# Value buffers initialised ahead of every load, sink rows filled ahead of the queued loads, weights loaded behind blocks 4 and 5

## Chip, cores, metric

One core of one Trainium2 chip. The metric is device microseconds of one execution. Single executions of one kernel spread by 1 to 4%. A run more than 1.5% above the fastest of its kernel counts as slow, and kernels are compared by their fast runs alone: ratios are the mean time of one kernel's fast runs over that of the other's of the same rounds. The medians quoted beside them are of all runs, so they do not give quite the same ratios. q3, k8 and the like are the loads of q or k of that block.

## The reference

Windowed attention with four sink positions, then a highway layer. q, k and v are 4 batches x 8 heads x 768 positions x 64, in float32.

```python
scores = scale * np.matmul(q, k.transpose(0, 1, 3, 2))
keep = is_sink | in_window                 # key < 4, or 0 <= query - key < 128
a = softmax(np.where(keep, scores, -1e9))
x = np.matmul(a, v)  ->  (3072, 512)       # heads side by side
H = np.maximum(x @ w_h, 0.0)
T = 1.0 / (1.0 + np.exp(-(x @ w_t + b_t)))
out = T * H + (1.0 - T) * x
```

## The kernel before

The 3072 rows are 24 blocks of 128, six to a batch. Every load casts float32 to float16 on its way and is issued by GpSimd. GpSimd's program runs up to eight blocks ahead of TensorE (`AHEAD = 8`); each engine runs its own list in order.

```python
# buffers of v: 12 of them; a column of 2.0 and a zero tail are written once, the rest by loads
for vt in v_ring[0:3]:
    init_v(vt)                              # VectorE, at the start
...
# GpSimd: loads 0, 1, 2 between the masks, then
load_sink_v(0)                              # 4 KB: v of the 4 sink positions
load_qk(3); load_v(3)
dma(wt_sb, moe_w_t); dma(wh_sb, moe_w_h)    # 512 KB each in SBUF
load_qk(4); load_v(4)
...
for i in range(-2, NB + LAG + 1):           # LAG = 4
    if i == -2:
        more_constants(); late_constants()
        for vt in v_ring[3:NV]:             # the other 9 buffers: VectorE
            init_v(vt)
        sink_ones(); sink_v(0)
    ...
    pe_T(i + 2)                             # TensorE transposes q and k: waits for their loads
    pe_A(i)                                 # e times v, and for blocks 2 to 5 of a batch the sink rows
    dve_x(i); sp_X(i)                       # x, then its transpose by DMA
    pe_Mt(i - LAG); pe_Mh(i - LAG)          # highway matmuls
    pe_sink(i + 1)                          # scores of sink keys (ks), blocks 2 to 5 of a batch, every other i
    # GpSimd: loads of block i+10 (5 to 8 at i == -2)
    load_qk(n); load_v(n)
    if (i + 2) % 6 == 0: pool_sink(...)     # GpSimd copies the batch's 4 sink keys into ks
    if i % 6 == 3: load_sink_v(next batch)
    if i % 6 == 0: sink_v(i // 6)           # GpSimd spreads the sink rows of v into vs
```

The softmax here doesn't subtract the row's maximum and nothing guards it: scores larger than these inputs give would overflow.

Of the kernel before, what the change touches and what calls it, by code (L numbers as in the profile page):

```python
# [8 lines left out]
FP16 = mybir.dt.float16  # L9
# [11 lines left out]
def kernel(  # L21
# [18 lines left out]
    nc = tc.nc  # L40
    P = 128

    B, H, S, D = q.shape
# [8 lines left out]
    NSC = S // P  # L52
# [3 lines left out]
    NOC = DM // P  # L56
    SCALE = 1.0 / math.sqrt(D)
    VW = H * 65 + 64
    AHEAD = 8
    LAG = 4  # L60

    const = ctx.enter_context(tc.tile_pool(name="const", bufs=1))
    sd_pool = ctx.enter_context(tc.tile_pool(name="p_sd", bufs=AHEAD))
# [3 lines left out]
    x_pool = ctx.enter_context(tc.tile_pool(name="p_x", bufs=LAG + 3))  # L67
# [4 lines left out]
    m_ps = ctx.enter_context(tc.tile_pool(name="ps_m", bufs=2, space=bass.MemoryType.PSUM))  # L72

    NV = AHEAD + 4
    v_ring = [const.tile([P, VW], FP16, tag=f"v{i}", name=f"v{i}") for i in range(NV)]
    qk_sd = {}

    def load_qk(n):
        b, c = divmod(n, NSC)
        rows = slice(c * P, (c + 1) * P)  # L80
        qsd = sd_pool.tile([P, H, D], FP16, tag="qsd", name="qsd")
        ksd = sd_pool.tile([P, H, D], FP16, tag="ksd", name="ksd")
        nc.gpsimd.dma_start(out=qsd, in_=q[b, :, rows, :].transpose([1, 0, 2]))  # L83
        nc.gpsimd.dma_start(out=ksd, in_=k[b, :, rows, :].transpose([1, 0, 2]))  # L84
        qk_sd[n] = (qsd, ksd)

    def load_v(n):
        b, c = divmod(n, NSC)
        rows = slice(c * P, (c + 1) * P)
        vt = v_ring[n % NV][:, 0:H * 65].rearrange("p (h e) -> p h e", e=65)  # L90
        nc.gpsimd.dma_start(out=vt[:, :, 0:D], in_=v[b, :, rows, :].transpose([1, 0, 2]))  # L91

    def init_v(vt):
        nc.vector.memset(vt[:, 0:H * 65].rearrange("p (h e) -> p h e", e=65)[:, :, D:D + 1], 2.0)  # L94
        nc.vector.memset(vt[:, H * 65:VW], 0.0)

    warm = const.tile([P, DM], FP16, tag="warm")
    ident = const.tile([P, P], FP16, tag="ident")
# [5 lines left out]
    wh_sb = const.tile([P, NOC, DM], FP16, tag="wh")  # L104
    wt_sb = const.tile([P, NOC, DM], FP16, tag="wt")
# [10 lines left out]
    with tc.manual_schedule(engines={ENG.DVE}):  # L116
        nc.vector.memset(warm, 0.0)
        nc.vector.memset(ident, 1.0)
        nc.vector.memset(ebias, _EXP_BIAS)
        nc.vector.memset(mask, 1.0)  # L120
        nc.vector.memset(bm, 1.0)
        for vt in v_ring[0:3]:
            init_v(vt)

    def load_sink_v(b):
        nc.gpsimd.dma_start(out=vs_dn[b % 2], in_=v[b, :, 0:4, :])

    def sink_v(b):
        nc.gpsimd.tensor_tensor(  # L129
            out=vs_bd[b % 2][0:NS4, :, 0:D], in0=vs_dn[b % 2].unsqueeze(1).to_broadcast([NS4, H, D]),  # L130
            in1=bm[0:NS4, :].unsqueeze(2).to_broadcast([NS4, H, D]), op=ALU.mult)

    with tc.manual_schedule(engines={ENG.Pool}):
        load_qk(0)
        nc.gpsimd.affine_select(
            out=ident, in_=ident, compare_op=ALU.is_equal, fill=0.0,
            base=0, pattern=[[-1, P]], channel_multiplier=1)
        load_v(0)
        load_qk(1)
        nc.gpsimd.affine_select(  # L140
            out=mask[:, 1, :], in_=mask[:, 1, :], compare_op=ALU.is_ge, fill=0.0,
            base=0, pattern=[[1, P]], channel_multiplier=-1)
        load_v(1)
        nc.gpsimd.affine_select(
            out=mask[:, 0, :], in_=mask[:, 0, :], compare_op=ALU.is_ge, fill=0.0,
            base=-1, pattern=[[-1, P]], channel_multiplier=1)
        load_qk(2)
        nc.gpsimd.affine_select(
            out=bm, in_=bm, compare_op=ALU.is_ge, fill=0.0,
            base=0, pattern=[[-4, H]], channel_multiplier=1)  # L150
        nc.gpsimd.affine_select(
            out=bm, in_=bm, compare_op=ALU.is_ge, fill=0.0,
            base=3, pattern=[[4, H]], channel_multiplier=-1)
        load_v(2)
        load_sink_v(0)
        load_qk(3)
        load_v(3)
        nc.gpsimd.dma_start(out=wt_sb, in_=moe_w_t.rearrange("(kc p) of -> p kc of", p=P))
        nc.gpsimd.dma_start(out=wh_sb, in_=moe_w_h.rearrange("(kc p) of -> p kc of", p=P))
        load_qk(4)  # L160
        load_v(4)

    nc.sync.dma_start(out=bt32, in_=moe_b_t.unsqueeze(0))

# [24 lines left out]
            nc.tensor.matmul(w, lhsT=warm[:, 0:P], rhs=warm, start=True, stop=True)  # L189

    qkT, tp_of, s_of, e_of, av_of, rec_of = {}, {}, {}, {}, {}, {}
    xh_of, xT_of, t_of, u_of, h_of, dd_of, ee_of, sk_of = {}, {}, {}, {}, {}, {}, {}, {}

    def pe_T(n):
        qsd, ksd = qk_sd.pop(n)
        tp = m_ps.tile([P, 2 * NHP, P], FP16, tag="m", name="tp")
        for j in range(NHP):
            nc.tensor.transpose(tp[:, j, :], qsd[:, 2 * j:2 * j + 2, :], ident)
        for j in range(NHP):
            nc.tensor.transpose(tp[:, NHP + j, :], ksd[:, 2 * j:2 * j + 2, :], ident)  # L200
        tp_of[n] = tp

    def act_T(n):
        qk = qkT_pool.tile([P, 2 * NHP, P], FP16, tag="qk", name="qk")
        nc.scalar.copy(out=qk, in_=tp_of.pop(n))  # L205
        qkT[n] = (qk[:, 0:NHP, :], qk[:, NHP:2 * NHP, :])

    def pool_sink(b):
        _, kT = qkT[b * NSC]
        ks = ks_bd[b % 2]  # L210
        for hh in range(2):
            rows = slice(64 * hh, 64 * hh + 64)
            dst = ks[rows, 0:NHP * 136].rearrange("p (a b) -> p a b", b=136)
            nc.gpsimd.tensor_copy(out=dst[:, :, 4 * hh:4 * hh + NSINK],
                                  in_=kT[rows, :, 0:NSINK])
# [87 lines left out]
    def sp_X(n):  # L303
        xT = x_pool.tile([P, NOC, P], FP16, tag="xT", name="xT")
        nc.sync.dma_start_transpose(out=xT, in_=xh_of[n])
        xT_of[n] = xT

    def pe_Mt(n):
        xT = xT_of[n]
        tps = m_ps.tile([P, DM], FP32, tag="m", name="tps")  # L310
        nc.tensor.matmul(tps, lhsT=ones_row, rhs=bt16, start=True, stop=False)  # L311
        for kc in range(NOC):
            nc.tensor.matmul(tps, lhsT=xT[:, kc, :], rhs=wt_sb[:, kc, :],  # L313
                             start=False, stop=(kc == NOC - 1))
        t_of[n] = tps
# [26 lines left out]
    def dve_o(n):  # L342
# [2 lines left out]
                                       op0=ALU.mult, op1=ALU.add)  # L345
        nc.sync.dma_start(out=out[n * P:(n + 1) * P, :], in_=otok)

    def on(n):
        return 0 <= n < NB

    with tc.manual_schedule(engines={ENG.PE, ENG.DVE, ENG.Activation, ENG.SP, ENG.Pool}):
        for i in range(-2, NB + LAG + 1):
            m, o = i - LAG, i - LAG - 1
            if i == -2:
                warm_up(8)
                more_constants()
                late_constants()
                for vt in v_ring[3:NV]:
                    init_v(vt)
                sink_ones()  # L360
                sink_v(0)
            if on(i) and i % NSC >= 2 and i % 2 == 0:
                act_sink(i)
            if on(i + 1):
                pe_S(i + 1, 0)
                act_S(i + 1, 0)
                pe_S(i + 1, 1)
            if on(o):
                dve_d(o)
            if on(i):  # L370
                dve_mask(i, 1)
            if on(i + 2):
                pe_T(i + 2)
            if on(o):
                dve_e(o)
            if on(i):
                pe_A(i)
            if on(i + 2):
                act_T(i + 2)
            if on(i + 1):  # L380
                act_S(i + 1, 1)
                dve_mask(i + 1, 0)
            if on(i):
                dve_rec(i)
            if on(o):
                dve_o(o)
            if on(i):
                dve_x(i)
                sp_X(i)
            if on(m):  # L390
                pe_Mt(m)
                act_u(m)
                pe_Mh(m)
            if on(i + 1) and (i + 1) % NSC >= 2 and (i + 1) % 2 == 0:
                pe_sink(i + 1)
            first, last = (5, AHEAD) if i == -2 else (i + 2 + AHEAD, i + 2 + AHEAD)
            for n in range(first, last + 1):
                if n < NB:
                    load_qk(n)
                    load_v(n)  # L400
            if on(i + 2) and (i + 2) % NSC == 0:
                pool_sink((i + 2) // NSC)
            b = i // NSC + 1
            if i >= 0 and i % NSC == 3 and b < B:
                load_sink_v(b)
            if i >= 0 and i % NSC == 0 and i > 0 and i // NSC < B:
                sink_v(i // NSC)


# [33 lines left out]
```

## Time and profile before

| | before |
|---|---|
| median of the runs beside the changed kernel | 148.12 us (147.62 to 149.33) |
| span of the profiled run | 144.5 us |
| busy: TensorE, VectorE, ScalarE, GpSimd | 76, 67, 60, 52% of the span |
| block 0 multiplied with v (av) from | 28.2 us |

Two rows of the page's picture in 40 slices show where TensorE stands still. A digit is the busy share of a slice of 3.6 us in tenths; PEclk is the granted clock.

```profile
span 144.5 us, 3130 instructions
PE   6645000190799999989999994899999999979930
PEclk9999999999999999999999999999999999999998
```

Counted from 1, slices 5 to 7, with zeros, and slice 8 are the hole from 14 to 28 us that the change is after; the 0 and 7 in slices 10 and 11 are the wait for sink keys. The rest is read in the prediction.

### The profile page before, as it was taken

Reading aid. Unit: us, or ns where it says so; the run is one execution under the profiler, and the core shown is the slowest. Engines: PE = TensorE matmul, PEld = TensorE weight load, DVE = VectorE, ACT = ScalarE, POOL = GpSimd, SP = SyncE. Lnnn points to the kernel's source line nnn. Section 1 sums busy time; section 2 is a strip of 40 time slices with the busy share of each in tenths; the row PEclk is TensorE's granted clock in tenths of the full one; section 3 lists DMA queues with packets and bytes.
Section 4 is the critical chain, followed back from the end, with each engine's and each line's share of the span. In section 5 each row is a group of like instructions: output and inputs, shape, how many; then the busy total and the mean of one; then the engine's idle time right before and its main releaser. Section 6 shows DMA issues by size and latency. Waiting matters only on the chain.

```text
span 144.5 us, 3130 instructions
## 1 busy us (share of the span) xinstructions
PE 109.9 (76%) x1216; PEld 70.4 (49%) x1216; DVE 97.0 (67%) x213; ACT 86.9 (60%) x105; POOL 75.8 (52%) x99
## 2 busy tenths in 40 slices
PE   6645000190799999989999994899999999979930
PEld 2234000180688566656765663567666666644400
DVE  6220000464066789988888995499889989988990
ACT  3058300061499869887886989198869888812210
POOL 6989980399999959876746479641030000000000
PEclk9999999999999999999999999999999999999998
DMA  1999999999999999999999999999943422634331
GB/s 11 111 134 105 119 173 169 86 96 147 160 156 155 153 134 194 196 186 163 179 187 187 182 185 161 140 178 195 185 119 109 113 90 79 54 111 128 126 145 73
DMA packets 92784, 20.14 MB, mean 139 GB/s; under 512 B 88673, under 2 KB 89697, under 8 KB 92770
## 3 DMA queue, kind: packets, MB, share of 16 engines
q0 software_dynamic: 76256, 10.51, 116.2%
q1 hardware_dynamic: 16514, 9.44, 31.3%
q8 instruction: 9, 0.15, 0.5%
q14 instruction: 5, 0.04, 0.1%
HBM read 21.01 MB, written 6.29 MB: 189 GB/s over the span
## 4 chain that ended last, share of the span: by engine, by line
PE 29%; POOL 25%; DMA 21%; issue 9%; DVE 8%; ACT 4%; POOLq 0%; DVEq 0%
DMA v<-in_v_dram 21%; POOL qsd L83 8%; POOL ksd L84 7%; PE tps L313 7%; PE hps L326 6%; POOL v L91 6%; PE av L279 6%; PE sps L245 3%; DVE dd L332 3%; DVE ee L338 2%; DVE otok L344 2%; ACT e L253 2%; PE av L285 2%; POOL vs L129 2%; PE tps L311 2%
## 5 line engine op out<-in xcount | busy, mean ns | idle before, releaser
L253 ACT ACTIVATE e<-sps,ebias 128x1024 f16<-128x1024 f32 (+1 forms) x48 | 49.8, 1042 | 19.8 <-PE sps L245 19.6
L279 PE MATMUL av<-v,e 128*128 128x112 f16 x352 | 25.4, 221 | 15.5 <-DVE e L264 15.5
L264 DVE TENSOR_TENSOR e<-e,mask 128x1024 f16<-128x1024 f16 (+1 forms) x48 | 31.1, 650 | 7.5 <-ACT e L253 7.1
L279 PEld LDWEIGHTS <-e 128*128 128x128 f16 x352 | 21.3, 102 | 21.0 <-DVE e L264 16.6
L205 ACT COPY qk<-tp 128x1024 f16<-128x1024 f16 x24 | 24.1, 1003 | 7.0 <-PE tp L200 7.0
L91 POOL DMA_DIRECT2D v<-in_v_dram x24 | 21.8, 910 | 10.2 <-DVE v L94 6.4
L84 POOL DMA_DIRECT2D ksd<-in_k_dram x24 | 21.7, 902 | 6.8 <-PE tps L313 3.4
L83 POOL DMA_DIRECT2D qsd<-in_q_dram x24 | 22.2, 925 | 4.9 <-DMA ksd<-in_k_dram 1.4
L326 PE MATMUL hps<-wh_sb,xT 128*128 128x512 f16 x96 | 24.6, 379 | 0.0
L313 PE MATMUL tps<-wt_sb,xT 128*128 128x512 f16 x96 | 24.6, 379 | 0.0
L319 ACT ACTIVATE u<-tps 128x512 f16<-128x512 f32 x24 | 14.4, 599 | 14.6 <-PE tps L313 14.6
L332 DVE SCALAR_TENSOR_TENSOR dd<-hps,xh 128x512 f16<-128x512 f32 x24 | 16.6, 690 | 7.4 <-PE hps L326 7.0
L245 PE MATMUL sps<-qk 64*128 64x128 f16 x352 | 16.0, 231 | 2.7 <-ACT qk L205 2.2
L338 DVE SCALAR_TENSOR_TENSOR ee<-u,dd 128x512 f16<-128x512 f16 x24 | 16.5, 686 | 0.5
L298 DVE TENSOR_TENSOR xh<-av,rec 128x512 f16<-128x512 f32 x24 | 16.4, 685 | 0.2
L245 PEld LDWEIGHTS <-qk 64*128 64x128 f16 x352 | 11.2, 100 | 9.9 <-issue 7.8
L344 DVE SCALAR_TENSOR_TENSOR otok<-xh,ee 128x512 f32<-128x512 f16 x24 | 15.6, 652 | 0.2
L326 PEld LDWEIGHTS <-xT 128*128 128x128 f16 x96 | 9.4, 98 | 11.8 <-issue 0.8
L313 PEld LDWEIGHTS <-xT 128*128 128x128 f16 x96 | 9.4, 98 | 9.2
L94 DVE MEMSET v<- 128x8 f16 x12 | 0.7, 65 | 18.4 <-DMA v<-in_v_dram 18.4
L285 PE MATMUL av<-vs,es 128*128 128x260 f16 x32 | 9.0, 281 | 3.3 <-POOL vs L129 3.3
L200 PE MATMUL tp<-ident,ksd 128*128 128x128 f16 x96 | 10.5, 238 | 1.1 <-DMA ksd<-in_k_dram 1.1
(45 smaller groups left out, 81.4 us busy)
## 6 DMA issues: line engine op xcount, KB each, us to landing
out_dram<-otok SPq DMA_DIRECT2D x24, 256.0 KB, 3.8
qsd<-in_q_dram POOLq DMA_DIRECT2D x24, 128.0 KB, 8.5
ksd<-in_k_dram POOLq DMA_DIRECT2D x24, 128.0 KB, 8.4
v<-in_v_dram POOLq DMA_DIRECT2D x24, 128.0 KB, 8.8
wt_sb<-in_moe_w_t_dram POOLq DMA_DIRECT2D x1, 512.0 KB, 7.6
wh_sb<-in_moe_w_h_dram POOLq DMA_DIRECT2D x1, 512.0 KB, 9.4
xT<-xh SPq DMA_TRANSPOSE x24, 7.0
vd<-in_v_dram POOLq DMA_DIRECT2D x4, 4.0 KB, 8.8
```

The costliest lines, as they stand in the source:

```text
L83: nc.gpsimd.dma_start(out=qsd, in_=q[b, :, rows, :].transpose([1, 0, 2]))
L84: nc.gpsimd.dma_start(out=ksd, in_=k[b, :, rows, :].transpose([1, 0, 2]))
L91: nc.gpsimd.dma_start(out=vt[:, :, 0:D], in_=v[b, :, rows, :].transpose([1, 0, 2]))
L205: nc.scalar.copy(out=qk, in_=tp_of.pop(n))
L245: nc.tensor.matmul(sps[:, hh, o:o + P], lhsT=kk[rows, hp, :], rhs=qT[rows, hp, :], start=True, stop=True)
L253: nc.scalar.activation(out=e.rearrange("p a b c d -> p a (b c d)"), in_=sps[:, :, 0:2 * np_ * P], func=AF.Exp, bias=ebias, scale=SCALE)
L264: nc.vector.tensor_tensor(out=ev, in0=ev, in1=m.unsqueeze(1).to_broadcast([P, 4, np_ * P]), op=ALU.mult)
L279: nc.tensor.matmul(av[:, g, 2 * hl + hh, 0:_AVN], lhsT=e[:, hh, hl, pc, :], rhs=vt[:, 65 * h:65 * h + _AVN], start=first, stop=False, skip ...
L313: nc.tensor.matmul(tps, lhsT=xT[:, kc, :], rhs=wt_sb[:, kc, :], start=False, stop=(kc == NOC - 1))
L326: nc.tensor.matmul(hps, lhsT=xT[:, kc, :], rhs=wh_sb[:, kc, :], start=(kc == 0), stop=(kc == NOC - 1))
L332: nc.vector.scalar_tensor_tensor(out=dd, in0=h_of.pop(n), scalar=0.0, in1=xh_of[n], op0=ALU.max, op1=ALU.subtract)
L338: nc.vector.scalar_tensor_tensor(out=ee, in0=u_of.pop(n), scalar=1.0, in1=dd_of.pop(n), op0=ALU.add, op1=ALU.mult)
```

## The change

The intent is to let VectorE through: no memset of a v buffer shall wait for a load into that buffer. Then TensorE needs the sinks early, so they are filled ahead of the loads that queue up, and the weights, needed only from block 0's highway step on, go behind blocks 4 and 5. (The diff also brings a way to transpose x on TensorE, which is switched off: `by_dma` is always true.)

```diff
+    WAT = 4
-        for vt in v_ring[0:3]:
+        for vt in v_ring:
             init_v(vt)
...
         load_v(2)
         load_sink_v(0)
-        load_qk(3)
-        load_v(3)
-        (wt_sb and wh_sb loaded)
-        load_qk(4)
-        load_v(4)
...
-                for vt in v_ring[3:NV]:
-                    init_v(vt)
                 sink_ones()
-                sink_v(0)
...
-            first, last = (5, AHEAD) if i == -2 else (i + 2 + AHEAD, i + 2 + AHEAD)
-            for n in range(first, last + 1):
+            if on(i + 2) and (i + 2) % NSC == 0:
+                pool_sink((i + 2) // NSC)
+                sink_v((i + 2) // NSC)
+            for n in (range(3, AHEAD + 1) if i == -2 else [i + 2 + AHEAD]):
                 if n < NB:
                     load_qk(n)
                     load_v(n)
-            if on(i + 2) and (i + 2) % NSC == 0:
-                pool_sink((i + 2) // NSC)
+                if n == WAT:      (wt_sb loaded)
+                if n == WAT + 1:  (wh_sb loaded)
             b = i // NSC + 1
-            if i >= 0 and i % NSC == 3 and b < B:
+            if i >= 0 and i % NSC == 1 and b < B:
                 load_sink_v(b)
-            if i >= 0 and i % NSC == 0 and i > 0 and i // NSC < B:
-                sink_v(i // NSC)
```

More of the change, by code (lines that the diff above doesn't have):

```diff
@@ L155 @@
         load_sink_v(0)
-        load_qk(3)
-        load_v(3)
-        nc.gpsimd.dma_start(out=wt_sb, in_=moe_w_t.rearrange("(kc p) of -> p kc of", p=P))
-        nc.gpsimd.dma_start(out=wh_sb, in_=moe_w_h.rearrange("(kc p) of -> p kc of", p=P))
-        load_qk(4)
-        load_v(4)
     nc.sync.dma_start(out=bt32, in_=moe_b_t.unsqueeze(0))
@@ L191 @@
     qkT, tp_of, s_of, e_of, av_of, rec_of = {}, {}, {}, {}, {}, {}
+    xtp_of = {}
     xh_of, xT_of, t_of, u_of, h_of, dd_of, ee_of, sk_of = {}, {}, {}, {}, {}, {}, {}, {}
@@ L306, in sp_X, with pe_X, act_X @@
         xT_of[n] = xT
+    def pe_X(n):
+        xh = xh_of[n]
+        xtp = m_ps.tile([P, NOC, P], FP16, tag="m", name="xtp")
+        for j in range(NOC):
+            nc.tensor.transpose(xtp[:, j, :], xh[:, j * P:(j + 1) * P], ident)
+        xtp_of[n] = xtp
+    def act_X(n):
+        xT = x_pool.tile([P, NOC, P], FP16, tag="xT", name="xT")
+        nc.scalar.copy(out=xT, in_=xtp_of.pop(n))
+        xT_of[n] = xT
     def pe_Mt(n):
@@ L346, in dve_o, with by_dma @@
         nc.sync.dma_start(out=out[n * P:(n + 1) * P, :], in_=otok)
+    def by_dma(n):
+        return True
     def on(n):
@@ L373 @@
                 pe_T(i + 2)
+            if on(i - 1) and not by_dma(i - 1):
+                pe_X(i - 1)
             if on(o):
@@ L379 @@
                 act_T(i + 2)
+            if on(i - 1) and not by_dma(i - 1):
+                act_X(i - 1)
             if on(i + 1):
@@ L388 @@
                 dve_x(i)
-                sp_X(i)
+                if by_dma(i):
+                    sp_X(i)
             if on(m):
@@ L400 @@
                     load_v(n)
-            if on(i + 2) and (i + 2) % NSC == 0:
-                pool_sink((i + 2) // NSC)
+                if n == WAT:
+                    nc.gpsimd.dma_start(out=wt_sb, in_=moe_w_t.rearrange("(kc p) of -> p kc of", p=P))
+                if n == WAT + 1:
+                    nc.gpsimd.dma_start(out=wh_sb, in_=moe_w_h.rearrange("(kc p) of -> p kc of", p=P))
             b = i // NSC + 1
-            if i >= 0 and i % NSC == 3 and b < B:
+            if i >= 0 and i % NSC == 1 and b < B:
                 load_sink_v(b)
-            if i >= 0 and i % NSC == 0 and i > 0 and i // NSC < B:
-                sink_v(i // NSC)
 _INS = ['q', 'k', 'v', 'n_sink', 'window', 'moe_w_h', 'moe_w_t', 'moe_b_t']
```

## The prediction

> **What bounds the kernel now.** I read the page, then the waits of the first 45 us, then the timeline of that stretch, then GpSimd's timeline to the end of its loads. The first four lines below are waits of 0 to 45 us (engine, line, what it waited for: us in total, times, longest); the rest are rows of the timeline (start us, length us, engine, line, operation, and in brackets the idle time before it with its releaser).
>
> ```profile
> DVE v L94 <- DMA v<-in_v_dram: 18.4, 2, 9.3
> PEld L279 <- DVE e L264: 15.0, 1, 15.0
> POOL v L91 <- DVE v L94: 6.4, 1, 6.4
> PE sk L223 <- POOL ks L214: 4.4, 1, 4.4
> ...
> 17.56 0.95 POOL L91 DMA_DIRECT2D v<-in_v_dram  x1
> 18.17 0.07 DVE L94 MEMSET v<- 128x8 f16 x1 [9.34 <-DMA v<-in_v_dram]
> ...
> 27.27 0.07 DVE L94 MEMSET v<- 128x8 f16 x1 [9.01 <-DMA v<-in_v_dram]
> ...
> 27.78 1.34 DVE L264 TENSOR_TENSOR e<-e,mask 128x512 f16<-128x512 f16 x3
> 28.24 0.69 PEld L279 LDWEIGHTS <-e 128*128 128x128 f16 x8 [14.99 <-DVE e L264]
> ```
>
> VectorE reaches the memsets of v buffers 3 to 11 at 8.8 us, but buffers 3 and 4 have loads under way into them by then, so it waits until load v3 lands (18.1) and load v4, which is queued behind both weights, lands (27.2). Only then does it mask the exponentials of block 0, which ScalarE had finished at about 9.3 and 12; TensorE waits 15 us for that mask. GpSimd in turn waits 6.4 us for the memset of v5, and its copies of the sink keys stand behind loads 5 to 8, which costs TensorE another 4.4 us. Block 0 thus starts its A matmuls at 28.24 and not near 13.5.
>
> The later part is different. The windows of 4 us show TensorE busy 4.00 of 4.00 in nearly all from 48 to 124, and a block takes about 4.1 us there (the tps groups start at 116.45, 120.52, 124.62, 128.63). But the queue of loads is full too, as GpSimd's rows show:
>
> ```profile
> 20.38 0.91 POOL L84 DMA_DIRECT2D ksd<-in_k_dram  x1
> 27.70 0.88 POOL L91 DMA_DIRECT2D v<-in_v_dram  x1 [6.40 <-DVE v L94]
> ...
> 64.79 0.88 POOL L84 DMA_DIRECT2D ksd<-in_k_dram  x1 [0.67 <-DMA v<-in_v_dram]
> ...
> 81.56 0.88 POOL L91 DMA_DIRECT2D v<-in_v_dram  x1 [1.86 <-DMA ksd<-in_k_dram]
> ...
> 89.64 1.03 POOL L129 TENSOR_TENSOR vs<-vd,bm 32x512 f16<-32x512 f16 x1
> ...
> 95.20 0.88 POOL L91 DMA_DIRECT2D v<-in_v_dram  x1 [1.62 <-DMA qsd<-in_q_dram]
> ```
>
> Eight loads can be under way (in the built program each load waits for the landing of the one eight before it), and between 60 and 96 GpSimd waits again and again for such a landing. Adding each issue's time to landing gives the supply: k8 lands at 40.4, k17 at 74.9, k23 at 102.7. So from k8 to k23 a block of loads takes 62.3/15 = 4.15 us, as much as TensorE needs. It does not hurt before the change because TensorE is late: it transposes block 8 at 53.5 (13 us after k8 landed) and block 23 at 118.8 (16 us after). **That lead is what the change will eat.**
>
> **What the Trainium skill says.** "Trainium Kernel Development and Optimization", Key Constraints: DMAs issued from SP, ACT and POOL run on the same 16 DMA engines and interleave; "DMA: Bandwidth & Descriptors", SWDGE vs HWDGE vs iDMA: each DMA engine round-robins between the queues that feed it. The trace agrees: alone but backlogged, loads land 0.85 us apart (24.49 to 28.73, five loads), beside transposes and stores 1.4 us apart (4.15/3). "DMA: Bandwidth & Descriptors", Anatomy of one DMA, gives a fixed cost of about 2.0 us; here the 4 KB load of sink rows took 3.07 us from issue to landing at the start, and that number is used. "TensorE: Matmul & The Clock Gate", Part 1, says that TensorE runs at half clock until it has been busy for some 3.4 us: here four transposes take 0.61 us up to 40 us and 0.40 us from 42 us on, though the granted clock is 1.00 throughout, so early blocks cost TensorE more (3.5 to 4.5 us).
>
> **The change part by part.**
>
> (a) All v buffers are initialised ahead of the loads. It moves nine pairs of memsets (about 0.06 us a pair in the row at 27.3 and after, 0.55 us) to about 1.8 us, where VectorE has 2.28 us to spare before the mask at 6.66. It removes the 18.4 us of VectorE's waits and the 6.4 us of GpSimd's. Block 0 can be multiplied at about 13.5 (after its block 2 transposes, 12.5 to 13.5). Up to 14.7 us are free here, if the loads follow.
>
> (b) Sink rows ahead of queued loads. The order of GpSimd's instructions in the changed program: the two copies of sink keys between the two selects on bm (9.45 to 9.94 before; qk of block 0 is done at 8.15, so no wait, 0.54 us), then v2, then the 4 KB load, then at once the sink-value multiply, which waits for that load. Issue of v2 about 10.8, of the 4 KB load 11.7, landing 11.7 + 3.07 = 14.8, multiply 1.12: GpSimd issues q3 at 16.0 rather than 11.70. **A new wait: 4.3 us in which no load is issued.** Later batches: the TensorE waits for the sink values (2.58 us at 90.7, 0.72 at 63.3) go, since the load is issued two blocks earlier and the multiply ahead of that iteration's loads.
>
> (c) Weights behind blocks 4 and 5. The weights took 24.49 - 18.09 = 6.4 us of the queue. Now q3..v4 come before them. I walk the queue with 0.88 us an issue, 3.9 us from issue to landing, 0.85 us a queued load and 3.2 us a weight: k3 lands at 20.9 (before: 16.7), k4 23.4 (26.2), first weight 27.5, k5 29.0 (28.7), second weight 32.5, k6 34.1 (34.8), k7 36.6 (37.4), k8 39.2 without company, about 41 with the transposes that now run beside it (40.4). **The supply is therefore about where it was;** only the lead is used.
>
> The sum: TensorE's order puts the transposes of block n+2 ahead of the A matmuls of block n, so it runs as k arrives: block 3 at 21, 4 at 23.5, 5 at 29, 6 at 34.5, 7 at 37.5, 8 at 41 against 53.5 before, 12.5 us earlier. From there it may go at 4.1 us (block 23 at 41 + 15*4.1 = 102.5) or as the loads arrive. The loads: 62.3 us as before from k8 to k23, plus the stores that now fall into this stretch. Before, 12 stores were issued in it; now stores of blocks 0 to 16, 17. A store costs about 0.65 us of the DMA engines, an estimate: in the tail, with stores alone, the windows give a share of 0.27 to 0.31 of 2.13 us a store. Five more are 3.3 us. Transposes: 16 in both. So k23 lands at 41 + 62.3 + 3.3 = 106.6. The later of the two, 106.6, sets the transposes of block 23, against 118.8. What follows that point (25.7 us to the end, TensorE and then VectorE) stays. Span 144.5 - 12 = 132.5; time 148.5 - 12 = **136.5 us**.
>
> **Rivals.** Rival 1, loads keep up, TensorE alone is the bound: block 23 at 102.5, time about 132.5. For it: TensorE is the busiest engine by the page, 76%; when TensorE waits, transposes and stores pause too and leave the DMA engines to the loads. Against it: 4.15 us a block of loads with few stores beside them. Rival 2, the supply is worse than I think: the gap of 4.3 us at 12 to 16 is not made up, and transposes and stores cost the loads more (the contended rate was 1.4 us a load, or 1.65 us a block over the 2.55 of the loads alone; with that figure and 90.8 us of work behind 18.8 us, k23 lands at 109.6). Time about 140, and the idle TensorE might fall back to its slow clock, 1 or 2 us more. Against: a wait of 2.58 us did not slow it before. Rival 3, the start was hidden anyway since TensorE or VectorE has a floor elsewhere: nothing gained, 148. Against: after 124 us the engines work on the last blocks without any wait for loads, so an earlier start of the pipeline moves the end with it. Rival 4, the new wait of GpSimd on the 4 KB load delays every load by 4.3 us and the weights late at 32.5 hold up the first highway matmuls: these come at iteration 4, near 35, so the weights land just in time; a miss costs a us or two.
>
> **Range and chances.** Rival 1 makes the lower end, 132, rival 2 the upper, 141; I add a little on both sides for run-to-run spread (147.7 to 149.3 before): 131.5 to 141.5. Slower needs a stall in the middle over 10 us, for which I see no cause. Faster by over 2%: 0.95; same 0.04; slower 0.01.
>
> **What would show it.** Right: no VectorE memset waits for a load; block 0's A matmuls at 13 to 15; GpSimd idle some 3 us ahead of the sink multiply near 15; TensorE waiting for ksd or qsd loads at blocks 3 to 8 and again in the middle; k23 landing at 104 to 110 with the transposes of block 23 right behind it; no TensorE wait for sink values at 60 to 90; 25 to 26 us from there to the end. Wrong: TensorE busy throughout from 41 with loads landing well ahead (then rival 1), k8 landing later than 44, or a long new wait of TensorE or ScalarE that is not for a load.

## The result and the profile after

The changed kernel takes 143.23 us (142.58 to 143.74, 4 runs) against 148.12; ratio 0.9656, 95% interval 0.958 to 0.973. It is faster, by less than half of what was predicted (136.5, with 131.5 as the low and 141.5 as the high end). Line numbers have moved: L194/L196 are the transposes of q and k, L219 the scores of sink keys, L210 GpSimd's copies of sink keys, L130 its multiply for sink values, L275 the av matmuls.

The same rows of the page after the change:

```profile
span 140.8 us, 3122 instructions
PE   6557439519599980499999999999999999979930
PEclk9955555995999998569999999999999999999995
```

The zeros at 14 to 28 us are gone, though the slices there are about half full, and there is a new hole at slices 16 and 17, that is, at 53 to 60 us. The waits of the whole run after the change (engine, line, what it waited for: us in total, times, longest) name both:

```profile
POOL vs L130 <- DMA vd<-in_v_dram: 13.0, 3, 10.0
...
PE tp L194 <- DMA qsd<-in_q_dram: 8.1, 5, 3.3
...
PEld L219 <- POOL ks L210: 6.5, 1, 6.5
PE sk L219 <- POOL ks L210: 6.0, 1, 6.0
...
PE tp L196 <- DMA ksd<-in_k_dram: 2.9, 5, 1.2
```

No memset of v is among them any more. TensorE waits 11 us for q and k, and 6.0 us, once, for sink keys. The timeline of the start shows the first part (start us, length us, engine, line, operation; in brackets the idle time before it and its releaser):

```profile
13.48 0.95 PE L275 MATMUL av<-v,e 128*128 128x112 f16 x8
...
14.62 1.03 POOL L130 TENSOR_TENSOR vs<-vd,bm 32x512 f16<-32x512 f16 x1 [2.77 <-DMA vd<-in_v_dram]
...
15.61 0.95 POOL L84 DMA_DIRECT2D qsd<-in_q_dram  x1
...
19.70 0.61 PE L194 MATMUL tp<-ident,qsd 128*128 128x128 f16 x4 [3.29 <-DMA qsd<-in_q_dram]
...
31.53 0.61 PE L194 MATMUL tp<-ident,qsd 128*128 128x128 f16 x4 [3.04 <-DMA qsd<-in_q_dram]
```

Block 0 is multiplied at 13.48, as predicted; GpSimd stands until the 4 KB load has landed and issues q3 at 15.61 (predicted 16.0). The timeline of the middle shows the second part:

```profile
54.54 0.87 POOL L85 DMA_DIRECT2D ksd<-in_k_dram  x1 [0.54 <-issue]
57.08 0.87 POOL L92 DMA_DIRECT2D v<-in_v_dram  x1 [1.67 <-DMA ksd<-in_k_dram]
57.95 0.45 POOL L210 COPY ks<-qk 64x16 f16<-64x16 f16 x2
...
58.45 1.03 PE L219 MATMUL sk<-qk,ks 128*128 128x128 f16 x8 [5.99 <-POOL ks L210]
```

The copy of batch 1's sink keys takes 0.45 us and its operand had been ready since about 39 (block 6 was transposed at 37.7, and ScalarE copied it at 38.2). It stands in GpSimd's list behind the loads of block 13, and v13 waited for the load eight before it: k11 landed at 56.78, and v13 was issued 0.30 us later. TensorE was at block 8 and needed those keys at 52.5. Before the change the same copy and the same scores stood like this, with the keys there before TensorE needed them:

```profile
54.82 1.22 POOL L214 COPY ks<-qk 64x16 f16<-64x16 f16 x2
...
60.45 0.61 PE L223 MATMUL sk<-qk,ks 128*128 128x128 f16 x8
```

After its wait TensorE was also slower for a while: from 58.4 to 61.9 us the granted clock was 0.50, and block 10 was transposed 1.93 us after the scores began. In the second run, which waited less (below), that took 1.11 us.

To follow the chain I take from the traces when a k block landed (issue start plus time to landing) and when TensorE began to transpose a block's q. What follows block 23's transposes, 25.7 to 26.0 us, is the same in all runs.

| us | k8 landed | block 8 | block 10 | k23 landed | block 23 | end |
|---|---|---|---|---|---|---|
| before | 40.4 | 53.5 | 61.5 | 102.7 | 118.7 | 144.5 |
| predicted | 41 | 41 | - | 106.6 | 106.6 | 132.5 |
| changed | 44.0 | 45.6 | 60.4 | 109.3 | 115.0 | 140.8 |
| changed, second run | 46.0 | 48.8 | 59.7 | 109.6 | 115.7 | 141.6 |

Eight us of gain at block 8 are down to one at block 10. After that TensorE waits only 0.9 us in all until the end, for a mask: 54.6 us for the 13 blocks from 10 to 23, 4.2 us a block.

### The profile page after: what moved, and what is told of

It is laid out like the page before. It is cut to its first block, busy times and chain, and to the rows that moved or that the text cites. A ratio compares the mean times of both kernels' runs of the same rounds, so it can differ in the third digit from the quotient of the medians.

```text
span 140.8 us, 3122 instructions
## 1 busy us (share of the span) xinstructions
PE 111.8 (79%) x1216; PEld 72.0 (51%) x1216; DVE 97.8 (69%) x213; ACT 87.4 (62%) x105; POOL 75.6 (54%) x99
## 3 DMA queue, kind: packets, MB, share of 16 engines
q0 software_dynamic: 76256, 10.51, 117.5%
## 4 chain that ended last, share of the span: by engine, by line
DMA 33%; POOL 28%; issue 14%; PE 13%; DVE 8%; POOLq 1%; DVEq 0%
DMA ksd<-in_k_dram 16%; DMA qsd<-in_q_dram 9%; POOL qsd L84 8%; POOL ksd L85 7%; POOL v L92 6%; DMA v<-in_v_dram 6%; PE av L275 3%; PE hps L334 3%; PE tps L321 3%; DVE dd L340 3%; DVE ee L346 2%; DVE otok L352 2%; DMA vd<-in_v_dram 2%; POOL vs L130 2%; POOL ks L210 2%
## 5 line engine op out<-in xcount | busy, mean ns | idle before, releaser
L275 PE MATMUL av<-v,e 128*128 128x112 f16 x352 | 26.2, 225 | 0.9 <-DVE e L260 0.9
L275 PEld LDWEIGHTS <-e 128*128 128x128 f16 x352 | 22.1, 105 | 3.0 <-DVE e L260 2.0
L327 ACT ACTIVATE u<-tps 128x512 f16<-128x512 f32 x24 | 14.4, 599 | 11.9 <-PE tps L321 11.7
L346 DVE SCALAR_TENSOR_TENSOR ee<-u,dd 128x512 f16<-128x512 f16 x24 | 17.3, 720 | 0.5
L194 PE MATMUL tp<-ident,qsd 128*128 128x128 f16 x96 | 10.6, 240 | 8.1 <-DMA qsd<-in_q_dram 8.1
L289 DVE RECIPROCAL rec<-av 128x8 f32<-128x8 f32 x24 | 4.8, 202 | 14.6 <-PE av L281 8.9
L196 PE MATMUL tp<-ident,ksd 128*128 128x128 f16 x96 | 10.5, 238 | 2.9 <-DMA ksd<-in_k_dram 2.9
```

The lines of the kernel that those rows point to most:

```text
L275: nc.tensor.matmul(av[:, g, 2 * hl + hh, 0:_AVN], lhsT=e[:, hh, hl, pc, :], rhs=vt[:, 65 * h:65 * h + _AVN], start=first, stop=False, skip ...
L346: nc.vector.scalar_tensor_tensor(out=ee, in0=u_of.pop(n), scalar=1.0, in1=dd_of.pop(n), op0=ALU.add, op1=ALU.mult)
```

## The experiments

Theory A: the wait for sink keys, made by their place behind loads in GpSimd's list, is what was missed. Theory B: the supply of loads holds the kernel, and without that wait TensorE would stand for loads instead. All runs gave correct results. The runs of before had medians of 147.9 to 149.6.

**Keys alone on VectorE.**

```diff
-            nc.gpsimd.tensor_copy(out=dst[:, :, 4 * hh:4 * hh + NSINK],
+            nc.vector.tensor_copy(out=dst[:, :, 4 * hh:4 * hh + NSINK],
```

> The changed kernel with the copies of sink keys moved from GpSimd to VectorE; all else as changed. Theory A (what the prediction missed is a wait of TensorE for sink keys that GpSimd copies only after it has issued the loads of block 13, each held back by the landing of the load eight before): the wait of 5.99 us at 58.45 vanishes, block 10 is transposed near 53.5 and not 60.4, span about 134.5, time about 137.2. Theory B (the supply of loads binds as soon as that wait is gone: k12 landed at 60.7 only 1 us before TensorE would want it, and it landed so early because TensorE stood still): TensorE waits for q or k of blocks 10 to 16 instead, 2 to 4 us in all, time 139 to 141. If neither wait matters: 143.

143.04 us (140.28 to 146.39), ratio 0.958, interval 0.939 to 0.976: too wide to tell from the changed kernel. The profiled run fell in the slow state, so only the kind of its waits is read. This is a line of its waits:

```profile
PE av L281 <- POOL vs L130: 5.5, 2, 3.8
```

L281 is the av matmul with the sink values. The wait for keys is gone and one for values stands in its place. The multiply for them is in the same list; in the longer of the two waits (3.84 us, at 88.25) it stood for its own 4 KB load, which landed at 87.09. Neither theory's number came out; the median is that of the third case (143), but the two fast runs had 142.37 and 140.28. The experiment took only the keys off the list.

**Keys and values on VectorE.** GpSimd is left with loads only; the 4 KB loads are issued two batches ahead.

```diff
-            nc.gpsimd.tensor_copy(...)  # keys         -        nc.gpsimd.tensor_tensor(...)  # values
+            nc.vector.tensor_copy(...)                 +        nc.vector.tensor_tensor(...)
         load_sink_v(0)
+        load_sink_v(1)
...
-                sink_v((i + 2) // NSC)      # moved to the end of the first block of a batch, on VectorE
```

> Sink keys and sink values both on VectorE, the 4 KB loads two batches ahead, so that GpSimd issues loads only. Theory A: no wait of GpSimd for the 4 KB load at 11.9 to 14.6 and no multiply of 1.03 us, so q3 is issued near 11.5 rather than 15.61 and the loads up to block 8 land about 4 us earlier (k7 at 37 instead of 41.2): time about 133.5 to 134.5. Theory B: the early loads gain 4 us, but loads bind later; time 136 to 139. If the hold at 12 to 16 was made up by the full queue anyway: same as the kernel with the keys alone moved.

133.98 us (133.36 to 134.43), ratio 0.908, interval 0.902 to 0.914, 5.8% below the changed kernel's ratio. Theory A's number was met: k8 landed at 40.1 and block 8 followed at 41.8. But this removes the hold at the start (in the changed kernel GpSimd stands from 11.9 to 14.6 us for the 4 KB load, then multiplies) as well as the wait in the middle, and loads begin to hold TensorE (0.55 and 1.28 us at 85 and 90), so the next two take the two apart.

**The hold alone.** The first sink values are filled behind the loads of block 4 again.

```diff
                 pool_sink((i + 2) // NSC)
-                sink_v((i + 2) // NSC)
+                if i >= 0:
+                    sink_v((i + 2) // NSC)
...
+                if n == 4:
+                    sink_v(0)
```

> The changed kernel with the first sink values filled behind the loads of block 4 again, so the hold of GpSimd at the start is taken out but the sink keys stay in its queue. If the hold is worth its 3.8 us and the later wait for keys is tied to the landings: everything shifts by about 3.5 us, time about 139.5, and the wait of TensorE for keys stays near 6 us. If the later wait for keys swallows what the earlier start gives: time 142 to 143 with a wait of 8 us or more.

140.22 us (139.81 to 143.19), ratio 0.949, interval 0.944 to 0.955. Everything came some 4 us earlier (k8 at 39.8, block 8 at 41.5, the copy of keys at 54.0) and the wait for keys stayed, 6.11 us. So the hold costs 1.6% by the ratios, about 2.4 us (3.0 by the medians), and the copy of keys moves with the landings.

**The middle wait alone, with values.** Batch 0 as changed, batches 1 to 3 on VectorE; their values are multiplied at the end of the first block of a batch, and their 4 KB loads are issued a batch earlier (not shown in the cut).

```diff
-            nc.gpsimd.tensor_copy(...)  # keys, values likewise
+            (nc.vector if b else nc.gpsimd).tensor_copy(...)
```

> The changed kernel with batch 0's sinks as they are (the hold of GpSimd near 12 to 16 stays) and keys and values of batches 1 to 3 on VectorE, with their 4 KB loads ahead. This takes out the middle wait alone, keys and values both. Theory A (the wait of 5.99 us in the middle is a term of the time by itself): 143.2 - 6.0 = 137.2. Theory B (loads bind once TensorE no longer stands still): 139 to 141, with waits of TensorE for q or k after block 8 adding up to 2 us or more.

140.83 us (139.07 to 144.39, 6 runs), ratio 0.946, interval 0.939 to 0.954. This is theory B's number. The wait for keys (6 us) is gone, but only 1.9% of the time is gained by the ratios, 2.8 us. TensorE now waits for k15 and k16, as its timeline shows:

```profile
77.24 0.40 PE L196 MATMUL tp<-ident,ksd 128*128 128x128 f16 x4 [1.50 <-DMA ksd<-in_k_dram]
...
82.94 0.40 PE L196 MATMUL tp<-ident,ksd 128*128 128x128 f16 x4 [1.21 <-DMA ksd<-in_k_dram]
```

Block 23 begins at 111.8, 1.6 us behind the landing of its k (110.2), where the changed kernel was 5.7 behind. In this version, too, GpSimd has one wait that the changed kernel has not: 1.9 us ahead of a 4 KB load, for VectorE.

**Another way to the same end: six blocks ahead instead of eight.** The sinks stay on GpSimd. `AHEAD` also sets the number of buffers: six instead of eight for q and for k, ten instead of twelve for v.

```diff
-    AHEAD = 8
+    AHEAD = 6
```

> The changed kernel with six blocks of loads ahead instead of eight; sinks stay on GpSimd. The copy of batch 1's keys then stands behind the loads of block 11 and not of block 13. Theory A (the place in GpSimd's queue makes the wait, not GpSimd's speed): the copy runs near 50, the wait of TensorE for keys falls from 6 us to under 1, and the time is that of the kernel with later sinks on VectorE, 139.5 to 141.5, the loads binding a little afterwards. Rival (fewer buffers hold the loads back): 143 to 146, with new waits of TensorE for q or k.

142.45 us (141.07 to 143.38), ratio 0.959, interval 0.949 to 0.970; the changed kernel in the same rounds had 142.97 and 0.9651. GpSimd reached the copy earlier, and TensorE never waited for keys:

```profile
50.72 0.46 POOL L210 COPY ks<-qk 64x16 f16<-64x16 f16 x2
```

So the place in the list makes the wait; GpSimd copies at the same speed (0.46 us). The time hardly moved: TensorE waited 6.9 us for q and 8.2 us for k in all, and block 23 waited for its k, which landed at 113.7 in this run. The time was outside what theory A gave for it, and outside the rival's as well.

**The initialisation alone, on the kernel before.**

```diff
-        for vt in v_ring[0:3]:
+        for vt in v_ring:
             init_v(vt)
...
-                for vt in v_ring[3:NV]:
-                    init_v(vt)
```

> The kernel before with the initialisation of all v buffers ahead of every load and nothing else. Theory A: VectorE's waits of 18.4 us vanish and block 0 is multiplied near 13.5, but the sink keys of the first batch now stand behind the loads of block 8, so TensorE waits for them until 32 to 34 (about 12 us from 20): start of that matmul 3 to 4 us earlier than before (36.96), time about 144 to 145. Rival (the initialisation is the whole of the gain): time 143 or less and no long wait for keys.

149.0 us (144.47 to 149.29) against 149.62 (147.23 to 150.86): unclear. The only fast run, 144.47, is where theory A had the time, but one run is too few. The profiled run was a slow one; its waits are of the kind that theory A named (in the line numbers of the kernel before, L223 and L214 are the scores and the copies of sink keys):

```profile
PE sk L223 <- POOL ks L214: 16.6, 1, 16.6
```

VectorE's wait for loads is gone, and TensorE waits as long for the keys of batch 0, which are copied behind the loads of block 8.

**The changed kernel with the sinks in the order of before.**

```diff
-            pool_sink(...) ; sink_v(...)        # ahead of the loads
+            pool_sink(...)                      # behind the loads; sink_v(0) behind block 4
```

> The changed kernel with keys and values of the sinks in the order of before (keys of batch 0 behind the loads of block 8, values behind block 4): buffers initialised early and weights later, part (b) undone. Theory A (the early initialisation only uncovers a wait for keys unless part (b) comes with it): TensorE waits for keys of batch 0 until 33 to 36, some 14 us or more, as in the kernel with the initialisation alone, and the time is 146 to 149, close to before. Rival (part (b) costs its hold of 3 us and gives little): 140 to 142.

146.21 us (143.26 to 147.23), ratio 0.975, interval 0.958 to 0.991. A line of its waits:

```profile
PE sk L219 <- POOL ks L210: 14.2, 1, 14.2
```

In the same rounds the changed kernel had 142.97 us and 0.9651, 0.956 to 0.974: the intervals overlap, so the times do not tell the two kernels apart, but the wait is plain. Without part (b) the early initialisation uncovers a wait of 14.2 us for keys; part (b) removes that wait and brings the hold. That part (b) pays in time is likely but not shown. (The 4 KB loads of later batches, too, are where they were before the change.)

**The weights behind block 3 again.** First on the changed kernel, then on the kernel with all sinks on VectorE.

```diff
-                if n == WAT:      (wt_sb loaded)
-                if n == WAT + 1:  (wh_sb loaded)
+                if n == 3:        (wt_sb and wh_sb loaded)
```

> The changed kernel with the weights loaded behind block 3 again, as before the change. Theory A (both orders put the same bytes in the queue ahead of block 6, and the wait for keys of batch 1 is tied to the landings of that queue): 142.5 to 144, that is, the same; k4 lands near 31 instead of 25.5, k6 near 37.5 as it was. Rival (loading the weights later is worth the 6 us that they take of the queue): 146 to 149.

142.62 us (140.48 to 144.23), ratio 0.952, interval 0.943 to 0.961.

> All sinks on VectorE and the weights behind block 3 again. Theory A: k4 and k5 land later, k6 and after as they were (33.9); block 6's transposes set the pace, so 133.5 to 135 against 134.0. Rival (weights late do matter once nothing else holds TensorE): 137 to 140, with TensorE waiting 6 us for block 4.

134.11 us (133.43 to 138.95), ratio 0.905, interval 0.898 to 0.914. Neither differs from its partner by more than the intervals allow (0.943 to 0.961 beside 0.958 to 0.973, and 0.898 to 0.914 beside 0.902 to 0.914); if anything, the first is the faster one. k4 lands later (30.6 and not 25.5 in the first), k8 does not (41.5 and not 44.0). Part (c) moves a wait, and no gain from it is shown here. (The second one's profiled run was a slow one.)

**The first six transposes of x on TensorE,** on the kernel with all sinks on VectorE, then on the changed kernel itself.

```diff
     def by_dma(n):
-        return True
+        return n >= 6
```

> All sinks on VectorE, and the transposes of the first six blocks of x on TensorE rather than by DMA. If a DMA transpose costs the loads about 1 us each (the supply walk came out 3 us early at k8 with 0.6 us a transpose; the packets of the loads thin out for 1 to 2 us at each transpose), k8 lands 3 to 5 us earlier than the 40.1 of the kernel with sinks on VectorE, and the time falls from 134.0 to 130 to 132. If the loads are held by something else: 134 or, for the added TensorE work of six blocks, 135 to 136.

130.84 us (130.56 to 131.16), ratio 0.884, interval 0.879 to 0.890: the fastest. k8 landed at 37.2 and not at 40.1, k23 at 98.0 and not at 104.6, and TensorE waits for no load after block 6.

> The changed kernel, sinks on GpSimd as changed, with the transposes of the first six blocks on TensorE. Theory A (the time at which GpSimd reaches the copy of batch 1's keys, 57.95 and about 58 in two runs of the changed kernel whether TensorE was at block 8 at 45.6 or at 48.8, is set by the landings of the loads ahead of it): with fewer transposes in the way the copy runs at 52 to 54, TensorE waits for it all the same (block 8 at 42 to 43), and the time is 138 to 140. If the copy's time is set otherwise, it stays at 58 and the time at 143.

136.83 us (136.1 to 139.08, 6 runs), ratio 0.925, interval 0.910 to 0.940. The landings moved (k8 at 40.4, k23 at 101.5) and the copy of keys moved with them, even further than expected, so that TensorE did not wait for keys:

```profile
49.62 0.89 POOL L92 DMA_DIRECT2D v<-in_v_dram  x1
50.49 0.59 POOL L210 COPY ks<-qk 64x16 f16<-64x16 f16 x2
```

A later wait, 2.69 us for the values of batch 3 at 105.7, was left.

**The changed kernel again,** in the rounds of the six-ahead and the sink-order runs.

> The changed kernel again, on the chip and in the rounds of the two others, so that they can be compared: 142.5 to 144, with the wait of TensorE for keys of batch 1 at 5 to 7 us.

142.97 us (142.58 to 143.28). TensorE was 3 us later at block 8 (48.8) and its wait for keys 3 us shorter (2.95, below what was expected), with the copy at 58.11 against 57.95: when block 10 begins is set by GpSimd's list and not by TensorE.

```profile
58.11 0.46 POOL L210 COPY ks<-qk 64x16 f16<-64x16 f16 x2
...
58.62 0.62 PE L219 MATMUL sk<-qk,ks 128*128 128x128 f16 x8 [2.95 <-POOL ks L210]
...
59.73 0.40 PE L194 MATMUL tp<-ident,qsd 128*128 128x128 f16 x4
```

The landings and block times of the runs, as in the table above (fast profiled runs only):

| us | k8 landed | block 8 | block 10 | k23 landed | block 23 | median time |
|---|---|---|---|---|---|---|
| first values late | 39.8 | 41.5 | 56.4 | 100.1 | 112.3 | 140.22 |
| later sinks on VectorE | 45.3 | 46.8 | 55.2 | 110.2 | 111.8 | 140.83 |
| six ahead | 45.8 | 48.1 | 56.3 | 113.7 | 113.5 | 142.45 |
| weights early | 41.5 | 45.9 | 56.2 | 104.3 | 112.9 | 142.62 |
| sinks on VectorE | 40.1 | 41.8 | 50.1 | 104.6 | 106.5 | 133.98 |
| the same, six transposes on TensorE | 37.2 | 40.4 | 49.5 | 98.0 | 103.7 | 130.84 |
| sinks in the order of before | 37.2 | 50.0 | 58.1 | 98.1 | 117.5 | 146.21 |
| changed, six transposes on TensorE | 40.4 | 43.5 | 52.6 | 101.5 | 110.4 | 136.83 |

## Why the prediction was wrong

Two steps failed. The path of TensorE lacked a wait for the sink keys of batch 1, which measured 5.99 us, and the supply of loads up to k8 was sized 3 to 5 us too short. The steps one by one:

- **Part (a), right.** "Block 0 can be multiplied at about 13.5": 13.48. No memset waited. That the lead of the loads over TensorE would be used up was right too: k8 had landed 13.1 us ahead of block 8 before, and 1.6 us ahead of it after.
- **Part (b) at the start, right.** q3 was foreseen at 16.0 and issued at 15.61. Taken away alone, this hold was worth 2.4 us of time.
- **Part (b) later on, wrong: a wait is missing from TensorE's path.** The prediction looked at the sink values of later batches ("the multiply ahead of that iteration's loads") and expected only waits to go. It did not ask where GpSimd would be in its list when TensorE, some 8 us earlier than before, came for the keys. Before the change the keys of batch 1 were copied at 54.8 and needed at 60.0. Now they were copied at 57.95 and needed at 52.5, which gives the 5.99 us. The signs of being wrong did cover it, as "a long new wait of TensorE or ScalarE that is not for a load", but no term of the sum did.
- **Part (c), wrong in size: the supply up to k8.** "The supply is therefore about where it was", with k8 at about 41: it landed at 44.0 and 46.0. Two terms were too small. First, the walk leaves out v5: by its own rates k5 lands at 29.2, v5 at 30.05, the second weight at 33.25 and k8 at 40.05, not at 39.2; the run without the first six transposes had 40.4. Second, the transposes of x were given 1.8 us up to k8. Five were issued by then in the changed kernel; without them k8 landed 3.6 us earlier (5.7 against the second run), and 2.9 earlier with the sinks on VectorE. The DMA packets of the kernel with the sinks on VectorE say the same: while the transpose at 40.5 to 42.5 ran, loads moved 131 KB less than at the 151 KB/us around it, which is about 0.9 us. Up to k23 the six transposes make 6.6 to 7.8 us (104.6 against 98.0, 109.3 against 101.5), more than six times 0.9, so some of that came by other ways.
- **From k8 to k23, near, but partly by luck.** 62.3 + 3.3 = 65.6 us was foreseen; the changed kernel had 65.3 and 63.6, the version without the middle wait 64.9. The terms differ, though: 15 stores and not 17 were issued in this stretch, and 14 or 15 transposes and not 16, while a store beside its transpose held back 238 to 257 KB of loads (44 to 60 us, same packets), about 0.8 us for the store and not 0.65. And with the first values late, though the later sinks were in the same order, the stretch took 60.3. Rival 2 had k23 at 109.6 and it came at 109.3; both of its reasons, the gap that is not made up and transposes that cost more, have runs on their side, and its slower TensorE after a wait was seen too.
- **"The later of the two sets the transposes of block 23", wrong.** Of the 8.4 us by which block 23 was late (115.0 against 106.6), 2.7 are k23 landing late and 5.7 are TensorE running behind k23; without the wait for sinks (later sinks on VectorE) it ran 1.6 behind. The two are not a sum of independent costs: by the ratios, taking the middle wait away gives back 2.8 us, since TensorE then runs into the supply; taking the hold away 2.4; taking both away 8.6. Mending one error alone takes the time to 140.83 (no wait for sinks in the middle) or to 136.83 (first six transposes off the DMA engines, which ended the wait for keys as well), where 136.5 was predicted.
- **After block 23, right.** 25.7 us were foreseen, 25.8 measured.
- **The time from the span.** The prediction took 12 us off the median of 148.5, and the profiled run before was 2.3 us faster than that median. The error in time is 6.7 us where that in the span is 8.3.

What stays open: why the stretch from k8 to k23 took 60.3 us in one kernel and 65.3 in another (two stores and one transpose fewer explain some 2.4 us, by the costs above); what the initialisation alone is worth, since its runs were too noisy to have a number; and whether part (b) pays in time.

## What to carry to other kernels

When a change lets the consumer start earlier, ask of each engine that works ahead where it will be in its list at that moment: small work that stands in a list of loads, behind loads that wait for landings, is as late as the landings. Take such work off the list that issues loads, all of it: with the keys alone moved, TensorE waited for the values. And once the consumer has used up its lead, look for what else rides on the DMA engines; here the transposes by DMA of the first six blocks were worth 3.1 us with the sinks moved, and about 6 without, where the wait for keys went with them.

## What the Trainium skill lacked or had wrong

- "DMA: Bandwidth & Descriptors", DMA Transpose (X-bar), gives no cost of a transpose beside loads. Here one of 128 x 512 float16 held back 131 KB of loads, about 0.9 us, as much as a whole load of 128 KB (0.85 us).
- The same page, SWDGE vs HWDGE vs iDMA, has no warning that compute in GpSimd's list waits for the landings that hold back its loads. Here a copy of 0.45 us came 5.99 us late for TensorE.
- "TensorE: Matmul & The Clock Gate", Seeing it yourself, says that the recorded clock events can be unreliable, and the run before the change agrees: four transposes took 0.61 us at 12.5 us, where the clock is given as full, and the same 0.61 us in the changed kernel at 31.5 us, where it is given as 0.50. It lacks a word on the mean that is made of them: 0.996 before and 0.89 after say nothing of which kernel's TensorE was slower.
